# Two transformer layers with attention: dense products in column tiles, half of the first shifted copies on GpSimd

## The chip, the core and the metric

One core of one Trainium2 chip runs the whole program in one launch. The time is the device time of an execution in microseconds; the kernel before was timed three times.

## What is computed

Four blocks in a row on x of 2048 tokens by 512 features, in bf16: attention, a feed-forward network, attention, a feed-forward network, each on a layer norm of x and added to x. Both layers use the same weights.

```python
def _A_ref(x, wqkv, wo):                      # 32 heads of 16 features
    q, k, v = split((x @ wqkv))               # scale 16 ** -0.5
    p = softmax(einsum("bhqd,bhkd->bhqk", q, k) * scale)
    return merge(einsum("bhqk,bhkd->bhqd", p, v)) @ wo
def _B_ref(x, w1, b1, w2, b2):                # 512 -> 1376 -> 512
    y = _layernorm(x)
    return gelu(y @ w1 + b1) @ w2 + b2
x = x + _A_ref(_layernorm(x), wqkv, wo)
x = x + _B_ref(_layernorm(x), w1, b1, w2, b2)
# ... and both once more
```

## The kernel before

**Work.** The queries are cut into units of 512 tokens (the last unit of the second layer into 256, 128 and 128), the heads into 8 groups of four. A unit and a head group make a segment, and a segment is a list of score tiles: 128 keys by 512 queries of one head. One tile fills one PSUM bank of 512 f32 columns.

**TensorE's three forms.** A head has 16 features, padded to 32 rows, so a score product (L1536) uses 32 of the array's 128 rows: four heads run side by side as row tiles. A product of exponentials with V (L1741) has 17 columns, 16 features and a row of ones that sums the denominator: four heads run side by side as column tiles and add up in one bank. The dense products use the whole array: QKV (L1016), output projection (L1821), both feed-forward products (L1882, L1943), and in the tail the last unit's second feed-forward product (L2004). The planner charges a switch between the forms (`PE_SWITCH`). Products of zeros (L1425 whole array, L1427 rows, L1429 columns) fill gaps.

**Two ways to an exponential.** Scores are scaled and shifted beforehand so that the integer part of their value is the bit pattern of a bf16 exponential. ScalarE takes groups of three and of two banks in turn and writes exponentials PT (L1521). VectorE takes single tiles: it reads the bank, adds a constant and converts to 16-bit integers dp, which read as bf16 are a rough exponential (the load, L1628). Two such tiles make a batch, 128 x 1024. The error is evened out by four copies of it, shifted by 0, 32, 64 and 96 in the bits, each multiplied with its own weighted V (vs). The copies are made on VectorE: the first adds 32 to the batch (L1659, 128x1024), the second adds 64 to both (L1667, 128x2048). Where two batches are ready at once one instruction does both (L1614 and L1615). So a tile on VectorE leaves four products with V to TensorE, one on ScalarE leaves one.

**GpSimd (POOL)** scales queries (L1262), writes the weighted V (L1287), applies layer norms (L951), squares keys (L1057), computes softmax bounds (L1095 to L1099) and merges the two parts of segments that are done in halves (L1784, L1792 to L1795).

**What sets the order.** When the kernel is built, a planner (`Sched.run`) keeps a clock for each engine. Jobs submit tasks with priorities and estimated durations; `best` picks for each engine the ready task with the best priority, and the order so found is written out as fixed instruction streams with semaphores. Each engine then runs its stream in order. Scores have priority 0; `scores_due` holds other products back when scores come due. `take_d` decides which tiles go to VectorE, by how much work is waiting there and by free buffers; lanes are bank 5 (`DLANE`) and bank 7 (`MISCB`). `try_pv` sizes the blocks of products with V, at most `PV_DEEP` = 2 rounds. A string (`Hint.ORDER`) sets a few planner constants anew for every fourth score group. For GpSimd and VectorE sharing, the planner adds to a "fast" VectorE task a fixed amount for each GpSimd task that overlaps it (`hits`).

**The tail.** After the last scores the last unit of 128 tokens goes through `job_tail`: its projection, its norm, L1882 with gelu on ScalarE (L2024) chunk by chunk, and L2004.

Of the kernel before, what the change touches and what calls it, by code (L numbers as in the profile page):

```python
# [24 lines left out]
DMA_MARGIN = 1.0  # L25

# [5 lines left out]
EPS = 1e-5  # L32
# [31 lines left out]
class Prog:  # L64


    def __init__(self):
# [11 lines left out]
        self.hits = []  # L79
# [26 lines left out]
    def op(self, eng, fn, reads=(), writes=(), same_ok=(), dur=0.3, lat=None):  # L106
# [12 lines left out]
        op.t0 = max(self.free[eng], self.ready(eng, reads, writes, same_ok))  # L119
        if eng == "sp":  # L120
# [158 lines left out]
class Sched:  # L279
# [102 lines left out]
    def task_ready(self, t):  # L382
        P = self.P
        r = 0.0
        for (fn, reads, writes, same_ok, dur, lat) in t.ops:
            x = P.ready(t.eng, reads, writes, same_ok)
            if x > r:
                r = x
        return r

    def best(self, e):
# [102 lines left out]
HOLD_LEAD = 0.45  # L494
FILL_GAP = 0.2
# [22 lines left out]
PV_DEEP = 2  # L518
# [40 lines left out]
class Builder:  # L559
# [45 lines left out]
    def alloc(self, es):  # L605
# [21 lines left out]
        self.cneg = t("cneg", [128, 4], F32)  # L627
        self.chalf = t("chalf", [128, 1], F32)
# [130 lines left out]
    def build_startup(self):  # L759
# [29 lines left out]
        pool(lambda e: e.memset(self.cneg[:, :], -0.5), [("cneg",)])  # L789
        pool(lambda e: e.memset(self.chalf[:, :], 0.5), [("chalf",)])  # L790
# [137 lines left out]
    def ln_group(self, tiles, slot, prio, eps1, eps0, shift):  # L928
# [12 lines left out]
        yield Task("pool", prio, [I(lambda e: e.tensor_scalar(out=rs, in0=var, scalar1=eps1, scalar2=eps0, op0=ALU.mult, op1=ALU.add), [("mv", c0 + i) for i in range(n)], [R], 0.2),  # L941
# [1225 lines left out]
```

## Time and profile before

| what | value |
|---|---|
| median of 3 runs | 1535.7 us (1535.5 to 1536.29) |
| the profiled execution, its span | 1535.9 us |
| instructions | 41170 |
| TensorE (PE), VectorE (DVE), ScalarE (ACT), GpSimd (POOL) busy | 97%, 94%, 98%, 22% |
| granted TensorE clock, mean | 0.999 |
| first exponential of scores, last one | 21.6 us, 1520.1 us |
| data moved by DMA | 90.55 MB, 59 GB/s |

The profiled execution has no time outside its span that these runs show: span and median differ by 0.2 us. In the rows that follow, a group stands with its line, engine and operation, the tile written and the tiles read, partitions by elements, the count, busy microseconds and mean nanoseconds of one, and the engine's idle time just before such instructions with what ended it. Instructions of one engine overlap a little at their ends, so a sum of durations is more than the busy time. TensorE's busy time includes the products of zeros, so 97% doesn't mean that it has no room. In a list of waits each row has the total, the number and the longest, in us. In a timeline a row begins with its start and its length in us.

### The profile page before, as it was taken

How to read it: one execution, taken by the hardware profiler on the slowest of the kernel's cores; microseconds unless marked ns; L12 is line 12 of the kernel's file. 1: busy time of each engine (PE TensorE's matmuls, PEld its weight loads, DVE VectorE, ACT ScalarE, POOL GpSimd, SP SyncE). 2: the span in 40 equal slices, each digit the busy share in tenths (PEclk: the TensorE clock that was granted, in tenths of full speed). 3: DMA queues.
4: the chain of work that ended last, by engine and by line, in shares of the span. 5: the costliest groups of instructions: out<-in, count | busy, mean ns of one | idle time of the engine just before them, and what ended most of it. 6: DMA issues, size and time to landing. Idle time of an engine off the chain costs nothing.

```text
span 1535.9 us, 41170 instructions
## 1 busy us (share of the span) xinstructions
PE 1486.8 (97%) x17654; PEld 491.3 (32%) x17654; DVE 1442.2 (94%) x2661; ACT 1502.5 (98%) x1346; POOL 343.0 (22%) x570
## 2 busy tenths in 40 slices
PE   9999999999999999999999999999999999999998
PEld 3222222222222222222322332222222222344555
DVE  8799999999999999999999899999999989998786
ACT  8999999999999999999999999999999999999897
POOL 3576321102120022202322138220002000020110
PEclk9999999999999999999999999999999999999999
DMA  6663102213312123214842332210011001120221
GB/s 163 120 154 91 32 22 34 51 35 68 82 48 63 37 64 84 56 35 100 138 69 64 60 87 63 53 30 18 22 36 35 14 27 32 36 49 18 73 67 30
DMA packets 212487, 90.55 MB, mean 59 GB/s; under 512 B 182251, under 2 KB 207184, under 8 KB 212304
## 3 DMA queue, kind: packets, MB, share of 16 engines
q1 hardware_dynamic: 212304, 87.92, 25.6%
q8 instruction: 138, 2.26, 0.6%
q14 instruction: 45, 0.37, 0.1%
HBM read 36.81 MB, written 19.48 MB: 37 GB/s over the span
## 4 chain that ended last, share of the span: by engine, by line
ACT 44%; PE 27%; DVE 24%; issue 3%; POOL 2%; DMA 0%; DVEq 0%; POOLq 0%
ACT PT L1521 41%; DVE dp L1628 10%; PE ps L1536 9%; PE ps L1741 8%; PE ps L1943 3%; DVE dp L1667 3%; PE ps L1882 2%; PE ps L1016 2%; ACT h L1934 2%; DVE dp L1615 2%; DVE dp L1659 1%; PE ps L1425 1%; DVE accT L1771 1%; DVE st L933 1%; DVE dp L1614 1%
## 5 line engine op out<-in xcount | busy, mean ns | idle before, releaser
L1521 ACT ACTIVATE PT<-ps 128x1536 bf16<-128x1536 f32 (+1 forms) x1256 | 1422.0, 1309 | 20.6 <-PE ps L1536 18.8
L1628 DVE TENSOR_SCALAR dp<-ps 128x512 uint16<-128x512 f32 x979 | 648.8, 679 | 33.7 <-PE ps L1536 30.4
L1536 PE MATMUL ps<-QT,KT 32*128 32x512 bf16 (+2 forms) x5120 | 602.6, 340 | 23.9 <-ACT PT L1521 7.5
L1741 PE MATMUL ps<-PT,V 128*17 128x512 bf16 (+2 forms) x3899 | 491.1, 338 | 0.6 <-issue 0.5
L1741 PE MATMUL ps<-dp,vs 128*17 128x512 bf16 (+2 forms) x3663 | 460.8, 339 | 2.7 <-issue 1.8
L1536 PEld LDWEIGHTS ps<-QT,KT 32*128 32x128 bf16 x5120 | 174.1, 91 | 543.6 <-ACT PT L1521 297.6
L1262 POOL TENSOR_SCALAR QT<-qraw,scl,qbias 128x512 bf16<-128x512 bf16 (+2 forms) x91 | 75.2, 827 | 762.8 <-PE ps L1536 754.3
L1741 PE MATMUL ps<-dp,V 128*17 128x512 bf16 (+2 forms) x1221 | 232.3, 340 | 1.6 <-DVE accT L1771 1.2
L1667 DVE TENSOR_SCALAR dp<-dp 128x2048 uint16<-128x2048 uint16 x310 | 214.3, 694 | 4.9 <-PE ps L1741 1.8
L1741 PEld LDWEIGHTS ps<-dp,vs 128*17 128x17 bf16 x3663 | 124.1, 89 | 114.1 <-issue 84.8
L1741 PEld LDWEIGHTS ps<-PT,V 128*17 128x17 bf16 x3899 | 126.9, 89 | 94.2 <-issue 75.1
L1429 PE MATMUL ps<-zw 128*32 128x448 bf16 (+23 forms) x1514 | 147.1, 322 | 0.1
L1659 DVE TENSOR_SCALAR dp<-dp 128x1024 uint16<-128x1024 uint16 (+1 forms) x298 | 126.1, 426 | 2.6
L1427 PE MATMUL ps<-zw 32*128 32x444 bf16 (+7 forms) x386 | 119.5, 332 | 0.0
L1615 DVE TENSOR_SCALAR dp<-dp 128x4096 uint16<-128x4096 uint16 x91 | 111.0, 1225 | 0.6 <-PE ps L1741 0.4
L1882 PE MATMUL ps<-yT,wf 128*128 128x512 bf16 (+5 forms) x440 | 102.7, 340 | 2.1 <-issue 1.0
L1016 PE MATMUL ps<-wqkv,xnT 128*128 128x512 bf16 x336 | 91.7, 382 | 4.1 <-DVE h L1029 1.1
L1425 PE MATMUL ps<-zw 128*128 128x448 bf16 (+14 forms) x347 | 87.4, 338 | 4.4 <-DVE onec L809 2.1
L1287 POOL TENSOR_SCALAR vs<-V 128x340 bf16<-128x340 bf16 (+2 forms) x72 | 64.3, 894 | 23.0 <-PE ps L1741 16.2
L1741 PEld LDWEIGHTS ps<-dp,V 128*17 128x17 bf16 x1221 | 58.2, 89 | 34.6 <-issue 19.4
L1614 DVE TENSOR_SCALAR dp<-dp 128x2048 uint16<-128x2048 uint16 x97 | 67.8, 700 | 0.0
L1771 DVE STREAM_TRANSPOSE accT<-ps 128x512 f32<-128x512 f32 (+2 forms) x96 | 59.2, 617 | 5.3 <-PE ps L1741 5.0
(201 smaller groups left out, 1053.4 us busy)
## 6 DMA issues: line engine op xcount, KB each, us to landing
vs<-vs_scr SPq DMA_DIRECT2D x64, 255.0 KB, 2.8
wf<-in_B_w_dram SPq DMA_DIRECT2D x90, 128.0 KB, 2.5
q_scr<-qk SPq DMA_DIRECT2D x20, 256.0 KB, 2.0
k_scr<-qk SPq DMA_DIRECT2D x12, 256.0 KB, 2.1
out_dram<-xres SPq DMA_DIRECT2D x16, 128.0 KB, 1.7
vs_scr<-vs SPq DMA_DIRECT2D x8, 255.0 KB, 3.3
xres<-in_A_x_dram SPq DMA_DIRECT2D x7, 256.0 KB, 5.3
v_scr<-vst SPq DMA_DIRECT2D x12, 136.0 KB, 1.7
```

The lines of the kernel that those rows point to most:

```text
L1016: yield Task("pe", prio if c0 == 0 else min(prio, HINT.LIN2), [I(lambda e, c=c: e.matmul(self.ps[:, b, :], lhsT=xnT[:, c, :], rhs=self.wqk ...
L1425: fn = lambda e: e.matmul(self.ps[:, b, 0:w], lhsT=self.zw[:, 0:128], rhs=self.zw[:, 0:w], start=st, stop=st, skip_group_check=True)
L1427: fn = lambda e: e.matmul(self.ps[:, b, 0:w], lhsT=self.zw[32 * p:32 * p + 32, 0:128], rhs=self.zw[32 * p:32 * p + 32, 0:w], start=st, sto ...
L1429: fn = lambda e: e.matmul(self.ps[32 * p:32 * p + 32, b, 0:w], lhsT=self.zw[:, 0:32], rhs=self.zw[:, 0:w], start=st, stop=st, skip_group_c ...
L1521: S_.submit(Task("act", 1e-5 * gi, [I(lambda e, pt=pt, n=n, b0=b0: e.activation(out=self.PT[:, pt:pt + n, :], in_=self.ps[:, b0:b0 + n, :] ...
L1536: return [I(lambda e, kb=kb, i=i: e.matmul(self.ps[:, b, i * W:(i + 1) * W], lhsT=self.KT[32 * hp:32 * hp + 32, hg, kb * 128:(kb + 1) * 12 ...
L1615: return lambda e: e.tensor_scalar(out=self.both(x[1], y[1]), in0=self.both(x[0], y[0]), scalar1=float(SHIFT[2]), scalar2=None, op0=ALU.add)
L1628: self.S_.submit(Task("dve", 0.0, [I(lambda e: e.tensor_scalar(out=self.dpu(u)[:, w * 512:(w + 1) * 512], in0=self.ps[:, b, :], scalar1=BI ...
L1659: t = Task("dve", prio(), [I(lambda e: e.tensor_scalar(out=self.dpu(u + 1)[:, 0:N], in0=self.dpu(u)[:, 0:N], scalar1=float(SHIFT[1]), scal ...
L1667: t = Task("dve", prio(), [I(lambda e: e.tensor_scalar(out=self.dpp(v)[:, :, 0:N], in0=self.dpp(u)[:, :, 0:N], scalar1=float(SHIFT[2]), sc ...
L1741: ops.append((nth[j, sh] + 0.1 * i, I(lambda e, hp=hp, v=v, ap=ap[:, i * W:(i + 1) * W], first=first and i == 0, W=W: e.matmul(self.ps[32 ...
L1882: yield Task("pe", self.soft(pr if c0 == 0 else min(pr, HINT.LIN2)) if y0 == 0 else pr, [I(lambda e, c=c: e.matmul(self.ps[0:M, b, 0:W], l ...
```

## The change

Three things change in what is computed where, and the planner that orders all of it changes with them.

1. **Dense products as four column tiles.** A new function `dense` writes one product of 128x128 weights as four products with 32 columns of the weights each, in the column form of the products with V, into the four quarters of the same bank. QKV beyond the first four token tiles, the output projection and both feed-forward products use it. The tail's projection and its second feed-forward product stay whole.
2. **TensorE stays in column tiles while scores can wait.** When the best task is scores and TensorE is in column form, `stay` looks for a column task that ends, with a switch, before the scores are due, and takes that first. Blocks of products with V can be up to 4 rounds deep in some hint modes.
3. **First shifted copies on GpSimd.** `shifter` gives the first copy of a full batch to GpSimd when GpSimd is free within 1.5 us and the segment has at least 12 tiles left; such a copy adds a constant of two 16-bit halves as 32-bit integers. The planner starts it behind VectorE's last "fast" task ("after"), and models a shared port: a fast task of VectorE and the body of a GpSimd task shut each other out.

Durations of many tasks are set anew, more VectorE tasks count as fast, the last unit of the first layer gets a better priority behind its attention, and `Hint.ORDER` is a new string over more modes.

```diff
@@ Prog.op
-                self.hits = self.hits[-3:] + [(op.t0, op.t0 + dur, lat or 0.0)]
+                if lat == "after" and self.dve_port[1] is not None:
+                    order = self.dve_port[1]
+                    op.t0 = max(op.t0, order.t1 + LATENCY["pool"])
+                body = max(op.t0 + POOL_HEAD, self.dve_port[0])
+                dur = body + max(0.0, dur - POOL_HEAD) - op.t0
+                if lat != "brief":
+                    self.pool_port = (body, op.t0 + dur)
...
-                dur += sum(h for t0, t1, h in self.hits if t0 < op.t0 + dur and op.t0 < t1)
+                body = op.t0 + DVE_HEAD
+                if self.pool_port[0] <= body:
+                    body = max(body, self.pool_port[1])
+                dur = body + dur - DVE_HEAD - op.t0
+                self.dve_port = (op.t0 + dur, op)
@@ Sched.task_ready
+            if lat == "fast":
+                r = max(r, P.pool_port[1] - DVE_HEAD)
+            elif lat == "after":
+                r = max(r, P.dve_port[0] + LATENCY["pool"])
@@ Sched.best
+            if e == "pe" and HINT.DEFER > -1 and self.P.tiling == "col" and (b.ops[0][5] or ("full",))[0] == "row":
+                c = self.stay(f, lim)
+                if c is not None:
+                    return c
+    def stay(self, f, lim):
+        P = self.P
+        act = P.free["act"] + sum(max(0.02, o[4] - OVERLAP["act"]) for t in self.pend["act"] for o in t.ops)
+        dve = P.free["dve"] + sum(o[4] for t in self.pend["dve"] if self.task_ready(t) <= f + D_NEAR for o in t.ops)
+        due = min(act - HOLD_LEAD + HINT.DEFER, dve - STAY_LEAD)
+        if f > due - 0.2:
+            return None
...
+            if r <= lim and self.drained(t, max(f, r)) + PE_SWITCH <= due:
...
@@ Hint
-    BASE = dict(D_IDLE=1.2, PV_LEAST=0.75, HOLD_LATE=0.4, PV_NEAR=0.7, LIN2=9, D_STEAL=0, POST=0)
+    BASE = dict(D_IDLE=1.2, PV_LEAST=0.75, HOLD_LATE=0.4, PV_NEAR=0.7, LIN2=9, D_STEAL=0, POST=0, POOL_SHIFT=1, PV_DEEP=2, DEFER=0.0)
...
@@ Builder
+POOL_SHIFT_US = 1.037
...
+        self.cstep = t("cstep", [128, 1], I32)
...
+        pool(lambda e: e.memset(self.cstep.bitcast(U16)[:, :], SHIFT[1]), [("cstep",)])
@@ job_d
+        eng = self.shifter(sg, n)
...
+                                       lambda e: e.tensor_tensor(out=self.dpu(u + 1).bitcast(I32), in0=self.dpu(u).bitcast(I32), in1=self.cstep[:, 0:1].broadcast_to([128, 512]), op=ALU.add),
...
+    def shifter(self, sg, n):
+        S_ = self.S_
+        if n < DBATCH or not HINT.POOL_SHIFT or self.left(sg) < PURGE:
+            return "dve"
+        near = S_.now + POOL_NEAR
+        if self.P.free["pool"] > near or any(S_.task_ready(t) <= near for t in S_.pend["pool"]):
+            return "dve"
+        self.npool += 1
+        return "pool"
@@ oproj_mm, and alike in mm, mm_w1 and job_ffn
+        if K == 128 and not tail:
+            return Task("pe", pr, [o for hp in hps for o in self.dense(b, lambda w, hp=hp: self.OT[:, hp, i * 128 + w.start:i * 128 + w.stop], lambda hp=hp: self.wo[:, hp, :], [("OT", hp)] + [("wo", k) for k in range(8)], hp == 0, hp == 3)])
...
+    def dense(self, b, lhsT, rhs, reads, start, stop, M=128, W=512):
+        return [I(lambda e, j=j: e.matmul(self.ps[32 * j:32 * j + 32, b, 0:W], lhsT=lhsT(slice(32 * j, 32 * j + 32)), rhs=rhs(), start=start, stop=stop, skip_group_check=True, tile_position=(0, 32 * j)),
+                  reads, [("ps", b)], 0.216 * W / 512, [("ps", b)], ("col", j)) for j in range(M // 32)]
```

The order of instructions shows what comes of it. In its rows stand the line, the operation, the tile written and those read, and the shape; "x" counts repeats. Lines after the change are higher by 48 to 69: scores L1584, products with V L1803, dense quarters L1890, the load L1676, the first copy L1708 on VectorE and L1709 on GpSimd, the second L1717.

First place: TensorE at a second feed-forward product of the first layer (wf, h: weights and hidden rows; QT, KT: scores). Before:

```order
L1943 MATMUL ps<-wf,h 128x512 x10
L1943 MATMUL ps<-wf,g 128x512
L1741 MATMUL ps<-dp,vs 17x512 x4
L1741 MATMUL ps<-dp,V 17x512
L1741 MATMUL ps<-dp,vs 17x512 x3
L1536 MATMUL ps<-QT,KT 128x512 x4
L1943 MATMUL ps<-wf,h 128x512 x2
L1536 MATMUL ps<-QT,KT 128x512 x2
L1943 MATMUL ps<-wf,h 128x512 x2
```

At the same product TensorE has now:

```order
L1890 MATMUL ps<-wf,h 32x512 x40
L1890 MATMUL ps<-wf,g 32x512 x4
L1803 MATMUL ps<-dp,vs 17x512 x3
L1803 MATMUL ps<-dp,V 17x512
L1584 MATMUL ps<-QT,KT 128x512 x2
L1803 MATMUL ps<-dp,vs 17x512 x8
L1890 MATMUL ps<-wf,h 32x512 x8
L1584 MATMUL ps<-QT,KT 128x512 x3
L1890 MATMUL ps<-wf,h 32x512 x8
```

Ten whole products are forty quarters now, and the step from the dense block to the products with V is no change of form any more.

Second place: VectorE in the middle of the first layer, with the semaphores that each instruction waits for (s_pe, s_pool, s_dve: TensorE, GpSimd, VectorE itself). Before:

```order
L1614 TENSOR_SCALAR dp<-dp 128x2x1024
L1659 TENSOR_SCALAR dp<-dp 128x1024 [waits s_dve]
L1628 TENSOR_SCALAR dp<-ps 128x512 [waits s_pe]
L1615 TENSOR_SCALAR dp<-dp 128x2x2048 [waits s_dve]
L1628 TENSOR_SCALAR dp<-ps 128x512 [waits s_dve,s_pe]
L1667 TENSOR_SCALAR dp<-dp 128x2048
```

VectorE after the change, at about the same place:

```order
L1717 TENSOR_SCALAR dp<-dp 128x2048 [waits s_pool]
L1676 TENSOR_SCALAR dp<-ps 128x512 [waits s_pe]
L1979 TENSOR_SCALAR h<-ps,b1c 128x512 [waits s_pe]
L1676 TENSOR_SCALAR dp<-ps 128x512 [waits s_pe] x4
L1717 TENSOR_SCALAR dp<-dp 128x2048 [waits s_pe,s_pool]
L1676 TENSOR_SCALAR dp<-ps 128x512 [waits s_pe] x2
```

First copies (L1659, L1614) have left VectorE's stream here, and second copies wait for GpSimd, with loads behind them in the stream.

Third place: TensorE in the tail, behind the last scores (L2004 before, L2071 after: the second feed-forward product). Before:

```order
L2053 MATMUL ps<-ident,xn 128x128 x4
L1943 MATMUL ps<-wqkv,g 128x512
L1882 MATMUL ps<-yT,wf 128x128 x16
L2004 MATMUL ps<-wqkv,h 128x512
L1882 MATMUL ps<-yT,wf 128x128 x2
```

In the tail TensorE has now:

```order
L2120 MATMUL ps<-ident,xn 128x128 x4
L1890 MATMUL ps<-wqkv,g 32x512 x4
L1890 MATMUL ps<-yT,wf 32x128 x64
L2071 MATMUL ps<-wqkv,h 128x512
L1890 MATMUL ps<-yT,wf 32x128 x8
```

Here quarters and whole products alternate, so there are changes of form where there were none.

More of the change, by code (lines that the diff above doesn't have):

```diff
@@ L25 @@
 DMA_MARGIN = 1.0
+POOL_HEAD = 0.2
+DVE_HEAD = 0.137
 LOG2E = 1.4426950408889634
@@ L119, in op @@
         op.t0 = max(self.free[eng], self.ready(eng, reads, writes, same_ok))
+        order = None
         if eng == "sp":
@@ L162, in op @@
                 add_dep(d, w)
+        if order is not None:
+            deps[id(order)] = order
         op.deps = list(deps.values())
@@ L494 @@
 HOLD_LEAD = 0.45
+STAY_LEAD = -0.3
+PV_OPEN = 0.25
 FILL_GAP = 0.2
@@ L1056, in job_qkv_tile @@
         eng = "pool" if what == "kv" else "dve"
-        yield Task(eng, prio, [I(lambda e: e.tensor_tensor(out=sq, in0=v4, in1=v4, op=ALU.mult), [("qk", qs, k) for k in range(k0, k1)], SR, 0.14 + 0.00845 * N if eng == "dve" else 1.04)])
+        yield Task(eng, prio, [I(lambda e: e.tensor_tensor(out=sq, in0=v4, in1=v4, op=ALU.mult), [("qk", qs, k) for k in range(k0, k1)], SR, 0.14 + 0.00845 * N if eng == "dve" else 1.04, (), "fast" if eng == "dve" else None)])
         if "k" in what:
@@ L1658, in job_d @@
         prio = lambda: 0.15 if not self.left(sg) and sg is self.segs[self.acc_seg] else 0.5 if self.left(sg) < DURGE else 2.5
[L1659 to L1661 removed]
+        eng = self.shifter(sg, n)
+        t = Task(eng, prio() if eng == "dve" else 0.6, [I((lambda e: e.tensor_scalar(out=self.dpu(u + 1)[:, 0:N], in0=self.dpu(u)[:, 0:N], scalar1=float(SHIFT[1]), scalar2=None, op0=ALU.add)) if eng == "dve" else
+                                       lambda e: e.tensor_tensor(out=self.dpu(u + 1).bitcast(I32), in0=self.dpu(u).bitcast(I32), in1=self.cstep[:, 0:1].broadcast_to([128, 512]), op=ALU.add),
+                                     ([] if eng == "dve" else [("cstep",)]) + [("dp", u, w) for w in range(n)], [("dp", u + 1, w) for w in range(n)] + self.dres(u + 1), 0.150 + 0.2605e-3 * N if eng == "dve" else POOL_SHIFT_US, (), "fast" if eng == "dve" else "after")])
+        if n == DBATCH and eng == "dve":
             t.mate = (1, u, u)
@@ L1704, in try_pv @@
                 by[sg["tiles"][it[1]][1]].append(it)
-            value = lambda r: sum(min(r, len(v)) for v in by.values()) / (4.0 * (r + PV_COST))
-            r = max(range(1, PV_DEEP + 1), key=value)
+            cost = PV_OPEN if self.P.tiling == "col" and not self.pv_out else PV_COST
+            value = lambda r: sum(min(r, len(v)) for v in by.values()) / (4.0 * (r + cost))
+            r = max(range(1, HINT.PV_DEEP + 1), key=value)
             if value(r) < HINT.PV_LEAST and not self.starved and len(near) < sg["n"] - sg["sub"]:
```

84 lines of the change are left out of this document (45 added, 39 removed).

## The prediction

> **What bounds the kernel now.** I read the page first: its busy shares, the chain that ended last, and the costliest groups.
>
> ```profile
> span 1535.9 us, 41170 instructions
> ...
> PE 1486.8 (97%) x17654; PEld 491.3 (32%) x17654; DVE 1442.2 (94%) x2661; ACT 1502.5 (98%) x1346; POOL 343.0 (22%) x570
> ...
> ACT 44%; PE 27%; DVE 24%; issue 3%; POOL 2%; DMA 0%; DVEq 0%; POOLq 0%
> ...
> L1521 ACT ACTIVATE PT<-ps 128x1536 bf16<-128x1536 f32 (+1 forms) x1256 | 1422.0, 1309 | 20.6 <-PE ps L1536 18.8
> ```
>
> Three engines are above 90%. Which of them sets the time? The list of waits says:
>
> ```profile
> PEld ps L1536 <- ACT PT L1521: 297.6, 751, 0.8
> ...
> ACT PT L1521 <- PE ps L1536: 18.8, 48, 2.5
> ```
>
> TensorE waits 297.6 us for ScalarE to free score banks; ScalarE waits 18.8 us for scores. So ScalarE's exponentials set the pace, and the other engines matter where they make it wait or take tiles from it. Its rows, shapes apart:
>
> ```profile
> L1521 ACT ACTIVATE PT<-ps 128x1536 bf16<-128x1536 f32 x605 | 924.6, 1528 | 14.6 <-PE ps L1536 13.2
> L1521 ACT ACTIVATE PT<-ps 128x1024 bf16<-128x1024 f32 x651 | 712.5, 1105 | 5.9 <-PE ps L1536 5.7
> ```
>
> 605 exps of three banks and 651 of two are 3117 banks (tiles of 512 columns). Neighbouring exps overlap, so the price of a bank is the page's union: 1422.0 / 3117 = 0.456 us. The rest of the score tiles, 979 of them, go to VectorE. The stages differ:
>
> ```profile
> core 0: us, PE busy (x) PEld busy (x) DVE busy (x) ACT busy (x) POOL busy (x), PEclk, DMA share, GB/s
> 400.00:500.00 100.00, 98.70 (x948) 28.03 (x945) 98.79 (x174) 99.79 (x89) 18.63 (x33) 1.00 0.25 66
> ...
> 800.00:900.00 100.00, 98.63 (x955) 29.66 (x952) 90.69 (x165) 97.64 (x84) 22.64 (x39) 1.00 0.26 57
> ...
> 848.50:862.00 13.50, 13.50 (x103) 4.11 (x102) 6.94 (x12) 12.19 (x12) 0.00 (x0) 1.00 0.00 0
> ```
>
> Mostly ScalarE is over 99% busy. In a burst of dense products (848.5 to 862) TensorE is busy throughout, VectorE half idle, and ScalarE loses 1.3 us. ScalarE's waits in 39:200, 800:1000 and 1400:1521:
>
> ```profile
> ACT PT L1521 <- PE ps L1536: 3.9, 14, 0.6
> ...
> ACT PT L1521 <- PE ps L1536: 5.3, 10, 2.5
> ...
> ACT PT L1521 <- PE ps L1536: 5.2, 10, 2.1
> ```
>
> These three stages hold 14.4 of the 18.8 us.
>
> **Part 1: first shifted copies on GpSimd.** A batch of two tiles on VectorE is two loads (L1628), a first copy (L1659, or L1614 for two batches at once) and a second copy (L1667, L1615).
>
> ```profile
> L1628 DVE TENSOR_SCALAR dp<-ps 128x512 uint16<-128x512 f32 x979 | 648.8, 679 | 33.7 <-PE ps L1536 30.4
> L1667 DVE TENSOR_SCALAR dp<-dp 128x2048 uint16<-128x2048 uint16 x305 | 212.2, 699 | 4.9 <-PE ps L1741 1.8
> L1659 DVE TENSOR_SCALAR dp<-dp 128x1024 uint16<-128x1024 uint16 x293 | 124.7, 429 | 2.6
> L1615 DVE TENSOR_SCALAR dp<-dp 128x4096 uint16<-128x4096 uint16 x91 | 111.0, 1225 | 0.6 <-PE ps L1741 0.4
> L1614 DVE TENSOR_SCALAR dp<-dp 128x2048 uint16<-128x2048 uint16 x97 | 67.8, 700 | 0.0
> ```
>
> By the order of instructions 258 of some 490 full batches get their first copy from GpSimd. VectorE: loads +18 x 0.679 = +12.2; single first copies -144 x 0.429 = -61.8; joined ones -55 x 0.700 = -38.5; single second copies +50 x 0.699 = +35.0; joined ones -23 x 1.225 = -28.2; ten more short batches, at half of 0.429 + 0.699, +5.6. Sum -76 us: VectorE falls from 1442 to about 1366 us.
>
> What the end sees of this is only the tiles that leave ScalarE: 601 and 648 exps, 3099 banks, 18 fewer. **18 x 0.456 = -8.2 us.** The 76 us buy only 18 tiles because copies must now wait in turn; that is the cost side.
>
> GpSimd's new copy, 512 32-bit words with a broadcast second operand, is not in this trace. Near rows are a 16-bit product of 512 elements, and on f32 a product of 256 with a broadcast operand (L1792), an add of two full streams (L1795) and a product of 16 (L1793):
>
> ```profile
> L1057 POOL TENSOR_TENSOR h<-qk x2: 1035/1037/1039, 47.8 to 68.4; 128x512 bf16<-128x512 bf16 x2
> ...
> L1792 POOL TENSOR_TENSOR dp<-dp,dw x16: 614/621/1316, 108.9 to 974.4; 128x256 f32<-128x256 f32 x16
> ...
> L1795 POOL TENSOR_TENSOR accT<-accT,dp x16: 726/731/1775, 110.1 to 976.6; 128x256 f32<-128x256 f32 x16
> ...
> L1793 POOL TENSOR_TENSOR den<-den,dw x16: 214/220/1203, 109.4 to 975.5; 128x16 f32<-128x16 f32 x16
> ```
>
> From medians: broadcast, (621 - 220) / 240 = 1.67 ns an element, so 220 + 496 x 1.67 = 1.05 us; two streams, 2.13 ns, so 1.28 us. I take 1.05, the row of the same form, and keep 1.04 to 1.28. The plan in the code reckons with 1.037. GpSimd gets 258 x 1.05 = 271 us on top of 343, 40% of the span. It has room, but its queue is in order: query scaling, layer-norm rows and merges can wait one copy more. [...]
>
> The two engines also exclude each other. Fast VectorE copies against GpSimd's query scaling:
>
> ```profile
> 788.21 0.78 DVE L1659 TENSOR_SCALAR dp<-dp 128x1024 uint16<-128x1024 uint16 x1
> ...
> 787.94 0.77 POOL L1262 TENSOR_SCALAR QT<-qraw,scl,qbias 128x512 bf16<-128x512 bf16 x1 [13.20 <-PE ps L1536]
> ...
> 1333.84 1.28 DVE L1667 TENSOR_SCALAR dp<-dp 128x2048 uint16<-128x2048 uint16 x2
> ...
> 1333.87 1.60 POOL L1262 TENSOR_SCALAR QT<-qraw,scl,qbias 128x256 bf16<-128x256 bf16 x1 [10.69 <-PE ps L1536]
> ```
>
> At 788 GpSimd came first (ends 788.71) and the copy took 0.78 instead of 0.43. At 1333 the copies came first (end 1335.12) and GpSimd stretched to 1.60. So each of the 258 copies closes VectorE's fast copies out for up to a microsecond; loads from PSUM go on. The new order starts GpSimd right behind a fast copy and puts loads beside it, and 213 second copies wait outright for GpSimd. If one is late, the loads queued behind it wait, and TensorE waits for their lanes. With the order fitted to 1.037 I take +1 us at the end, bounds -1 (lanes free earlier) to +20 (rival C).
>
> **Part 2: dense products as four column tiles.** Around a dense burst:
>
> ```profile
> 847.32 2.33 PE L1943 MATMUL ps<-wf,h 128*128 128x512 bf16 x10
> 849.49 0.38 PE L1943 MATMUL ps<-wf,g 128*128 128x512 bf16 x1
> 849.80 0.40 PE L1741 MATMUL ps<-dp,vs 128*17 128x512 bf16 x4
> 850.02 0.38 PE L1741 MATMUL ps<-dp,V 128*17 128x512 bf16 x1
> ...
> 850.35 0.60 PE L1536 MATMUL ps<-QT,KT 32*128 32x512 bf16 x4
> ...
> 626.26 0.74 PE L1429 MATMUL ps<-zw 128*32 128x448 bf16 x12
> ```
>
> Ten dense products take 2.17, 0.217 each; four column tiles 0.22 (849.80 to 850.02); from one form to another 0.31 (849.49 to 849.80), so a switch costs 0.31 - 0.216 = about 0.095. The order has 2670 changes of form before and 2568 after: -102 x 0.095 = -9.7 us of TensorE, in the stages where ScalarE waits. Against it, 18 more VectorE tiles replace 18 products with V by 72: +54 / 4 x 0.22 = +3. Does a dense product keep 0.217 in quarters? Twelve zero products with 32-column weights run in 0.74: (0.74 - 0.36) / 2 = 0.19 a round for 448 columns. So yes. [...] Staying in column tiles while scores can wait (`stay`) moves scores late on purpose; they are still planned to land before ScalarE runs dry. Of the 14.4 us of waits I take **-3 us**, bounds -12 and +8.
>
> **Part 3: the tail.** Behind the last scores before, everything on TensorE has one form:
>
> ```profile
> 1527.38 1.07 PE L1882 MATMUL ps<-yT,wf 128*128 128x128 bf16 x16 [0.30 <-DVE yT L2055]
> ...
> 1528.28 0.38 PE L2004 MATMUL ps<-wqkv,h 128*128 128x512 bf16 x1
> 1528.49 0.28 PE L1882 MATMUL ps<-yT,wf 128*128 128x128 bf16 x2
> ```
>
> After, the first product is in column tiles and the second is not: 12 changes, 12 x 0.095 = 1.1, in a stretch where little hides it: **+1 us**. The step constant and the planner's new costs issue nothing that lies on the path: 0.
>
> **Sum.** -8.2 + 1 - 3 + 1 = -9.2 us. The profiled execution (span 1535.9) and the median of the runs (1535.7) differ by 0.2, so I predict **1526.5 us**.
>
> **Rivals.** Changes within 0.2% (3.1 us) can't be told from none.
> A, the forecast: 1519 to 1532.6. For it: ScalarE's rate is steady, and its instruction count is fixed by the order. Chance 0.62.
> B, the dense stages stop making ScalarE wait: -8.2 + 1 - 12 + 1 = -18.2, 1517.5. Against it: the longest waits (2.5, 2.1) look like chains at stage ends, not switches. Chance 0.10.
> C, slower: GpSimd's copy is nearer 1.28 than 1.037, and closes out the second copies. 258 x 0.24 = 62 us of lateness; if a third reaches ScalarE through lanes and scores, +20 instead of +1, and the dense waits don't shrink: -8.2 + 20 + 0 + 1 = +12.8, 1548.5. It decides from about a fifth of the 62 on, where 13 us use up the gain and 3.1 more. For it: the 213 direct waits, with loads queued behind them. Against it: the broadcast row and VectorE's freed 76 us. Chance 0.14. [...]
> D, the quarters don't keep pace: four weight loads of 0.095 one after another would make 0.38 of 0.217; the order has 4408 quarters of 512 columns, 1102 products, and 1102 x 0.163 = 180 us of TensorE where it is full; a third on the path gives 1526.5 + 60 = 1586. The row at 626.26 speaks against it. Chance 0.04.
>
> ```profile
> L1429 PEld LDWEIGHTS ps<-zw 128*32 128x32 bf16 x1514 | 53.0, 95 | 20.6 <-DVE dp L1628 2.8 <-issue 1.0 <-ACT PT L1521 0.8
> ```
>
> E, gains and new waits cancel: within 0.2%. Chance 0.10.
>
> **The numbers.** Faster is A and B, 0.72; same E, 0.10; slower C and D, 0.18. The range runs from 1513 (B with a little more) to 1541 (a C where some 12 us pass through); beneath lie 0.05, above about 0.13.
>
> **What would show it.** Right: exps 601 and 648, ScalarE busy near 1494; the new copy at 1.04 to 1.10; dense quarters at 0.22 a round; ScalarE's wait for scores about 16 us; VectorE busy below 1400. Wrong: VectorE's second copies waiting for GpSimd by more than 30 us, or ScalarE's wait for scores above 28.

## The result and the profile after

The changed kernel takes **1556.2 us** (median of 4 runs, 1552.1 to 1558.0), the kernel before 1536.0 beside it. The ratio is 1.0123, interval 1.0104 to 1.0142: slower by 1.2%, where 1526.5 was forecast, above the upper end of the range, 1541. The profiled execution has a span of 1553.9. Its page and two of its groups, in the columns that the prediction showed:

```profile
span 1553.9 us, 48864 instructions
...
PE 1486.7 (96%) x21441; PEld 516.9 (33%) x21447; DVE 1388.1 (89%) x2527; ACT 1499.9 (97%) x1339; POOL 602.6 (39%) x829
...
PE 32%; ACT 32%; DVE 23%; POOL 5%; issue 3%; DMA 2%; SPq 2%; POOLq 0%; DVEq 0%
...
L1569 ACT ACTIVATE PT<-ps 128x1536 bf16<-128x1536 f32 (+1 forms) x1249 | 1419.7, 1275 | 38.3 <-PE ps L1584 35.0
```

```profile
L1569 ACT ACTIVATE PT<-ps 128x1536 bf16<-128x1536 f32 x601 | 898.5, 1495 | 30.3 <-PE ps L1584 27.8
L1569 ACT ACTIVATE PT<-ps 128x1024 bf16<-128x1024 f32 x648 | 687.8, 1070 | 8.0 <-PE ps L1584 7.2
...
L1709 POOL TENSOR_TENSOR dp<-dp,cstep 128x512 int32<-128x512 int32 x258 | 268.1, 1039 | 662.7 <-DVE dp L1676 381.0 <-DVE dp L1717 163.0 <-DVE dp L1663 51.6
```

601 and 648 exps as forecast, and the new copy costs 1.039. But the exps' union fell by 2.3 us (1422.0 to 1419.7), not by 8.2: one exp now takes 1495 and 1070 where it took 1528 and 1105, because fewer of them start while the one before still runs (1128 instead of 1174, counted in the traces) and these overlap it by less (0.15 us instead of 0.19 on average). An exp that starts behind the end of the one before takes 1450 or 1024 ns in both traces. So scores that come a little later can leave no idle row and still cost overlap. VectorE shows the same: its instructions sum to 69 us less, its busy time falls by only 54, to 1388 and not 1366. ScalarE's share of the chain went from 44% to 32%. The list of waits says what else is late:

```profile
ACT PT L1569 <- PE ps L1584: 35.0, 63, 4.5
DVE dp L1676 <- PE ps L1584: 61.5, 88, 6.7
DVE dp L1717 <- POOL dp L1709: 5.8, 7, 1.2
```

ScalarE waits 35.0 us for scores (18.8 before; 16 was forecast), VectorE's loads 61.5 (30.4 before). VectorE's second copies wait only 5.8 us for GpSimd: rival C is not what happened.

Where was it lost? The order differs, so instants can't be compared, but work can: each of the 4096 score tiles is either a bank of an exp or a load on VectorE. Counting the ends of both in the two traces gives the time at which so many tiles were done, and how many of them VectorE did:

```
tiles done      930     1926    2092    2424    3752    4090   last exp   end
before, us    368.7    729.7   786.0   914.4  1381.0  1519.0    1521.2  1535.9
after, us     371.0    726.4   791.3   925.6  1389.9  1534.3    1537.1  1553.9
difference     +2.3     -3.3    +5.4   +11.2    +8.8   +15.3     +15.9   +18.0
VectorE's     202/205  442/459  484/489 556/561 901/920 979/997
```

At tile 1926 the change does what it should: 17 more tiles on VectorE, 3.3 us ahead. Then 14.5 us go between 725 and 925, where the second layer's attention begins (the third of the four blocks, called the third layer from here on), and 9 from tile 3752 to the end.

**Between 725 and 925.** The third layer's keys and values are reloaded from memory in SyncE's queue. The reload's rows of before and, in the second fence, of after:

```profile
740.51 9.30 SPq L1301 DMA_TRANSPOSE KT<-k_scr  x5
...
752.85 2.89 SPq L1303 DMA_DIRECT2D V<-v_scr  x2
```

```profile
761.70 7.55 SPq L1349 DMA_TRANSPOSE KT<-k_scr  x4
...
778.26 0.57 SPq L1351 DMA_DIRECT2D V<-v_scr  x1
...
786.45 8.13 SPq L1351 DMA_DIRECT2D V<-v_scr  x6
```

It begins 21 us later, though the exps are ahead. VectorE meanwhile runs almost dry (1.62 us busy in 12.2), and then GpSimd, TensorE and ScalarE wait in one chain. The columns are those of the prediction's table of stages; the first fence is of before at the same instants (though not at the same work), where VectorE is busy throughout, the others are of after:

```profile
771.00:783.20 12.20, 12.06 (x151) 3.71 (x148) 12.18 (x21) 12.20 (x12) 3.42 (x4) 1.00 0.65 102
...
800.00:820.00 20.00, 19.90 (x215) 5.88 (x216) 19.89 (x37) 19.98 (x18) 7.24 (x10) 1.00 0.27 62
```

```profile
771.00:783.20 12.20, 11.94 (x120) 4.55 (x120) 1.62 (x4) 11.35 (x11) 3.00 (x4) 1.00 1.08 182
...
800.00:820.00 20.00, 15.57 (x162) 3.92 (x162) 14.86 (x28) 14.65 (x14) 9.27 (x15) 0.83 0.28 66
```

```profile
808.60:812.00 3.40, 3.36 (x23) 0.55 (x23) 3.25 (x8) 2.18 (x2) 0.46 (x2) 0.50 0.34 77
```

```profile
803.40 2.28 POOL L1335 TENSOR_SCALAR vs<-V 128x204 bf16<-128x204 bf16 x3 [4.34 <-PE ps L1584]
805.63 0.40 POOL L1846 COPY dp<-accT 128x256 f32<-128x256 f32 x1
...
806.54 1.03 POOL L991 TENSOR_TENSOR rs<-rs,cneg 128x4 f32<-128x4 f32 x1
807.55 1.04 POOL L1709 TENSOR_TENSOR dp<-dp,cstep 128x512 int32<-128x512 int32 x1
```

```profile
808.64 0.60 PE L1803 MATMUL ps<-dp,vs 128*17 128x512 bf16 x2 [4.23 <-POOL dp L1709]
```

```profile
809.82 2.47 ACT L1569 ACTIVATE PT<-ps 128x1536 bf16<-128x1536 f32 x2 [4.51 <-PE ps L1584]
```

The shifted copy at 807.55 has no wait of its own. It stands in GpSimd's queue behind weighted values (L1335) that wait 4.34 us, and TensorE waits for the copy. After TensorE has stood, its granted clock is 0.50 from 808.6 to 812.0 (0.83 over the 20 us), and a product takes 0.60 instead of 0.38.

**Behind 1400.** Here the units have 256 and 128 tokens. TensorE's waits that nothing in the profile explains ("issue"), behind 1420 after, and in the second fence of before, behind 1405:

```profile
PE ps L1584 <- issue: 3.6, 4, 1.7
PE ps L1803 <- issue: 3.4, 5, 1.3
PE ps L1890 <- issue: 2.6, 4, 0.9
```

```profile
PE ps L1741 <- issue: 2.4, 2, 1.8
...
PE ps L1882 <- issue: 1.0, 1, 1.0
...
PE ps L1536 <- issue: 0.8, 1, 0.8
```

9.6 us in all against 4.2. Four of them, and the instructions of TensorE between two of them (products and weight loads with their counts):

```profile
1526.32 0.38 PE L1890 MATMUL ps<-yT,wf 128*32 128x128 bf16 x13 [0.94 <-issue]
...
1530.07 0.29 PE L1584 MATMUL ps<-QT,KT 32*128 32x128 bf16 x5 [0.69 <-issue]
...
1533.81 0.38 PE L1890 MATMUL ps<-yT,wf 128*32 128x128 bf16 x13 [0.85 <-issue]
...
1537.83 0.33 PE L1803 MATMUL ps<-PT,V 128*17 128x128 bf16 x9 [1.31 <-issue]
```

```profile
1530.10:1533.80 3.70, 2.86 (x128) 2.19 (x128) 2.49 (x8) 3.32 (x3) 0.00 (x0) 1.00 0.14 31
1533.80:1537.80 4.00, 2.71 (x128) 2.10 (x128) 0.92 (x3) 3.18 (x4) 0.00 (x0) 1.00 0.06 12
```

128 products and 128 weight loads each time, whatever the lines are: three times in a row TensorE stands after 256 instructions. Counted through TensorE's whole stream, all eight waits for issue over 0.6 us behind 1420 stand at the same place of successive 256s, to one instruction, and the 256 ahead of each had run in 2.5 to 3.3 us; one that ran in 3.04 us had no such wait. The four waits of the kernel before stand at one place too. No trace shows what TensorE waits for there: that it is for instructions is the author's estimate, from the place alone.

**Tail.** From the last exp to the end it takes 16.7 us, 14.6 before. Of these 2.1 us, 1.3 stand ahead of the first gelu, where ScalarE waits 4.91 us instead of 3.57, behind the wait for issue at 1537.83; the other 0.7 come between the chunks.

### The profile page after: what moved, and what is told of

Its sections match the earlier page's. It is cut to its first block, busy times and chain, and to the rows that moved or that the text cites. A ratio compares the mean times of both kernels' runs of the same rounds, so it can differ in the third digit from the quotient of the medians.

```text
span 1553.9 us, 48864 instructions
## 1 busy us (share of the span) xinstructions
PE 1486.7 (96%) x21441; PEld 516.9 (33%) x21447; DVE 1388.1 (89%) x2527; ACT 1499.9 (97%) x1339; POOL 602.6 (39%) x829
## 4 chain that ended last, share of the span: by engine, by line
PE 32%; ACT 32%; DVE 23%; POOL 5%; issue 3%; DMA 2%; SPq 2%; POOLq 0%; DVEq 0%
ACT PT L1569 30%; PE ps L1803 11%; PE ps L1584 11%; DVE dp L1676 10%; PE ps L1890 7%; DVE dp L1717 3%; POOL vs L1335 1%; DVE dp L1663 1%; PE ps L1477 1%; ACT h L2002 1%; DVE accT L1833 1%; DMA xnT<-xn 1%; DVE dp L1708 1%; DVE st L982 1%; PE ps L1473 1%
## 5 line engine op out<-in xcount | busy, mean ns | idle before, releaser
L1569 ACT ACTIVATE PT<-ps 128x1536 bf16<-128x1536 f32 (+1 forms) x1249 | 1419.7, 1275 | 38.3 <-PE ps L1584 35.0
L1676 DVE TENSOR_SCALAR dp<-ps 128x512 uint16<-128x512 f32 x997 | 659.8, 680 | 69.9 <-PE ps L1584 61.5
L1584 PE MATMUL ps<-QT,KT 32*128 32x512 bf16 (+2 forms) x5120 | 598.9, 341 | 27.4 <-DVE dp L1676 8.0
L1709 POOL TENSOR_TENSOR dp<-dp,cstep 128x512 int32<-128x512 int32 x258 | 268.1, 1039 | 662.7 <-DVE dp L1676 381.0
L1803 PE MATMUL ps<-PT,V 128*17 128x512 bf16 (+2 forms) x3878 | 501.6, 340 | 2.7 <-issue 2.4
L1803 PE MATMUL ps<-dp,vs 128*17 128x512 bf16 (+2 forms) x3726 | 483.9, 339 | 7.7 <-POOL dp L1709 4.9
L1584 PEld LDWEIGHTS ps<-QT,KT 32*128 32x128 bf16 x5120 | 172.4, 91 | 523.1 <-ACT PT L1569 257.9
L1717 DVE TENSOR_SCALAR dp<-dp 128x2048 uint16<-128x2048 uint16 (+1 forms) x370 | 253.1, 689 | 9.6 <-POOL dp L1709 5.8
L1803 PE MATMUL ps<-dp,V 128*17 128x512 bf16 (+2 forms) x1242 | 231.0, 340 | 2.7 <-DVE accT L1833 2.6
L1803 PEld LDWEIGHTS ps<-dp,vs 128*17 128x17 bf16 x3726 | 134.1, 89 | 138.3 <-issue 92.0
L1803 PEld LDWEIGHTS ps<-PT,V 128*17 128x17 bf16 x3878 | 134.9, 89 | 100.2 <-issue 78.6
L1477 PE MATMUL ps<-zw 128*32 128x448 bf16 (+17 forms) x1573 | 163.3, 329 | 0.1
L1475 PE MATMUL ps<-zw 32*128 32x444 bf16 (+3 forms) x391 | 122.1, 331 | 0.0
L1890 PE MATMUL ps<-yT,wf 128*32 128x512 bf16 (+2 forms) x1720 | 104.7, 339 | 5.9 <-issue 2.8
L1890 PE MATMUL ps<-wqkv,xnT 128*32 128x512 bf16 x1392 | 96.5, 381 | 3.8 <-DMA xnT<-xn 2.5
L1473 PE MATMUL ps<-zw 128*128 128x448 bf16 (+12 forms) x330 | 84.0, 340 | 4.0 <-DVE onec L858 2.1
L1663 DVE TENSOR_SCALAR dp<-dp 128x4096 uint16<-128x4096 uint16 x68 | 84.2, 1238 | 1.6 <-PE ps L1803 1.1
L1803 PEld LDWEIGHTS ps<-dp,V 128*17 128x17 bf16 x1242 | 59.5, 89 | 41.8 <-issue 17.6
L1335 POOL TENSOR_SCALAR vs<-V 128x340 bf16<-128x340 bf16 (+2 forms) x72 | 62.5, 869 | 21.0 <-DMA V<-v_scr 10.2
L1708 DVE TENSOR_SCALAR dp<-dp 128x1024 uint16<-128x1024 uint16 (+1 forms) x164 | 67.7, 418 | 1.1
```

Of the source, the lines that this page charges most:

```text
L1473: fn = lambda e: e.matmul(self.ps[:, b, 0:w], lhsT=self.zw[:, 0:128], rhs=self.zw[:, 0:w], start=st, stop=st, skip_group_check=True)
L1475: fn = lambda e: e.matmul(self.ps[:, b, 0:w], lhsT=self.zw[32 * p:32 * p + 32, 0:128], rhs=self.zw[32 * p:32 * p + 32, 0:w], start=st, sto ...
L1477: fn = lambda e: e.matmul(self.ps[32 * p:32 * p + 32, b, 0:w], lhsT=self.zw[:, 0:32], rhs=self.zw[:, 0:w], start=st, stop=st, skip_group_c ...
L1569: S_.submit(Task("act", 1e-5 * gi, [I(lambda e, pt=pt, n=n, b0=b0: e.activation(out=self.PT[:, pt:pt + n, :], in_=self.ps[:, b0:b0 + n, :] ...
L1584: return [I(lambda e, kb=kb, i=i: e.matmul(self.ps[:, b, i * W:(i + 1) * W], lhsT=self.KT[32 * hp:32 * hp + 32, hg, kb * 128:(kb + 1) * 12 ...
L1663: return lambda e: e.tensor_scalar(out=self.both(x[1], y[1]), in0=self.both(x[0], y[0]), scalar1=float(SHIFT[2]), scalar2=None, op0=ALU.add)
```

## Experiments

Two theories at the start. Theory 1, an assumption from the waits at every 256 instructions: quarters make TensorE's instruction stream too dense for its supply. Theory 2: the first copies sit in GpSimd's queue behind work that waits for a transfer. In all held-order runs the planner makes the same order, and the edit is applied to the finished list of instructions. Ratios are against the kernel before, run beside each.

**1. Quarters undone, in the order held.**

```
 def whole(ops):                        # on the finished order
+    four quarters of a group -> one matmul(ps[0:M, b, 0:W], ...)
     e1: where W < 512        e2: everywhere
```

> The changed kernel with its order held, but every dense product of 128 or 256 columns (the first products of the units of 256 and 128 tokens) issued whole again instead of as quarters: 132 fewer groups of four, 396 matmuls and 396 weight loads fewer, 11 more changes of form. Theory 1 (TensorE's instructions come in blocks of 256, and a block that runs in under about 3.5 us makes TensorE stand for about 1 us): the narrow quarters run through a block in about 2 us, so stalls over 0.6 us of TensorE behind 1420 fall from 10 to 5 or 6 and the kernel gains 3 to 6 us against the changed kernel, 1550 to 1553. Theory 2 (the time is lost where GpSimd's queue and late chains hold TensorE): no change by more than 2 us, 1554 to 1558.

> The changed kernel with its order held, but every dense product issued whole again. TensorE's instructions fall back to 17,694 products, changes of form rise from 2568 to 2816. Theory 1 in its wide form (the longer instruction stream costs everywhere): 5 to 12 us faster than the changed kernel, 1544 to 1551. Theory 2 (quarters are harmless and save changes of form): 248 x 0.095 = 24 us more TensorE time, of which a third to all comes through, 1563 to 1580.

e1: 1546.75, ratio 1.0067 (1.0050 to 1.0084). e2: 1552.66, 1.0102 (1.0075 to 1.0129). Theory 1 in its narrow form holds so far: 132 groups of quarters cost some 8 us, more than the 3 to 6 expected, and TensorE's waits for issue behind 1405 fall from 9.6 us to 2.0. The quarters' own work is not what costs: 64 narrow quarters take 1.08 us here, and the same 16 whole products took 1.07 (the prediction's row at 1527.38).

```profile
1544.61 1.08 PE L1890 MATMUL ps<-yT,wf 128*32 128x128 bf16 x64 [0.19 <-DVE yT L2122]
```

Theory 1's wide form isn't borne out: with the wide quarters gone too the kernel is slower than e1 by 0.35%, though the intervals overlap a little. Nor did e2 lose the 7 us or more that theory 2 gave it.

**2. Empty instructions in place of the quarters.**

```
-        ops[0][0].one = lambda e: e.matmul(...)
+        ops[0][0].one = lambda e: [e.nop() for _ in range(6)] and e.matmul(...)
```

> The changed kernel with its order held and narrow dense products whole, as before in the first experiment (1546.75), but six empty instructions ahead of each of the 132 whole products on TensorE, so that its instruction stream is as long as with quarters. Theory 1 (blocks of 256 instructions run dry): the stalls come back, 8 or more over 0.6 us behind 1420 about 3.5 us apart, and the kernel is back at 1553 to 1558. If it was the quarters' own work (weight loads, lanes, forms): it stays at 1545 to 1549. Should an empty instruction cost time of its own, TensorE's gaps grow by the same amount at each of the 132 places instead of in single stalls.

1549.36, 1.0083 (1.0057 to 1.0110). The trace has 48073 instructions, as in e1: none of the empty ones stands in it. If they did not reach the chip, this is e1 measured again, and it says nothing on the theory. So a longer stream without the quarters was not measured. Both together put the narrow quarters at 6 to 9 us in this order.

**3. Weighted values behind the copy.**

```
 def vs_behind_copy(ops):
+    three ops of L1335 and their store (L1342), planned ahead of the copy that runs at 807.55,
+    go behind that copy; nothing else moves
```

> The changed kernel with one move: the three weighted copies of V on GpSimd that wait for a late load near 803 us, and their store, stand behind the next layer-norm rows and the next shifted copy instead of ahead of them. Theory 2 (the shifted copy now sits in GpSimd's queue behind work that waits for a transfer, and TensorE and VectorE wait for it): ScalarE's wait of 4.51 at 809.82 goes below 1, TensorE's clock stays full there, and the kernel gains 4 to 7 us, 1549 to 1552. Theory 1 (instruction blocks): no change, 1554 to 1558. If something else is late by as much there, under 2 us gained.

1547.89, 1.0068 (1.0049 to 1.0087). The chain is cut:

```profile
800.78 1.04 POOL L1709 TENSOR_TENSOR dp<-dp,cstep 128x512 int32<-128x512 int32 x1
802.51 2.67 POOL L1335 TENSOR_SCALAR vs<-V 128x204 bf16<-128x204 bf16 x3 [0.69 <-DMA vs_scr<-vs]
```

```profile
810.14 4.62 ACT L1569 ACTIVATE PT<-ps 128x1536 bf16<-128x1536 f32 x4 [1.33 <-PE ps L1584]
```

ScalarE's 4.51 is gone, 1.33 is left, and the granted clock is 1.00 there. From tile 1926 to 2424 the kernel now takes 195.5 us instead of 199.2, so the place itself is worth 3.7; the rest of e3's 8 us is spread over the run. The row at 802.51 holds a hint: GpSimd's wait is here put down to the *store* of weighted values, not to a load.

**4. Quarters alone, in the order of before.**

```
 def four(ops):                         # before.py, on the finished order
+    one dense matmul -> four quarters
     e4: all        d1: where W < 512        d2: where W == 512
```

> The kernel before with its order held, and only the dense products issued as quarters: 17,654 products become 21,419, changes of form fall from 2670 to 2565. If quarters are a gain as the prediction has it (105 x 0.095 = 10 us of TensorE time, a third at the end): 1531 to 1535. Theory 1 in its narrow form (blocks of 256 run dry in the narrow units): the gain is eaten there, 1535 to 1540, with more stalls over 0.6 us behind 1400 than the 5 of before. Theory 1 in its wide form: slower, 1541 to 1550.

> The kernel before with its order held and only the narrow dense products (128 and 256 columns) as quarters. Changes of form 2673 against 2670, so nothing is saved. If narrow quarters cost time by running blocks of instructions dry: 1538 to 1542, with the loss behind 1400. If they cost only in the changed kernel's order: 1535 to 1538, no change.

> The kernel before with its order held and only the dense products of 512 columns as quarters. Changes of form 2564 against 2670: 106 x 0.095 = 10 us of TensorE time saved. If the 8 us that all quarters cost there (1544.49) was the narrow ones: 1531 to 1536. If the longer stream costs in the wide stretches too, or if what was saved there is worth nothing and late transfers come on top: 1538 to 1545.

e4: 1544.49, 1.0048 (1.0033 to 1.0062). d1: 1541.37, 1.0025 (1.0012 to 1.0037). d2: 1537.97, 1.0000 (0.9985 to 1.0014). This is the cleanest answer of the study: wide quarters save 106 changes of form, by the prediction's estimate of 0.095 each (from the rows at 849.49 and 849.80) 10 us of TensorE, and the kernel gains nothing; narrow ones save nothing and cost 0.25%. In d2 ScalarE waits 19.3 us for scores where it waited 18.8, and TensorE waits for ScalarE to free banks 312.0 us where it waited 297.6: where ScalarE sets the pace, TensorE's saved time has no taker.

```profile
PEld ps L1536 <- ACT PT L1521: 312.0, 783, 0.8
ACT PT L1521 <- PE ps L1536: 19.3, 42, 2.5
```

All quarters together cost 0.48%, more than the parts' 0.25% and nothing; where the rest comes from stays open.

**5. Both repairs, and all late dense products whole.**

```
 c1: whole (W < 512) and vs_behind_copy
 c2: whole (all dense products planned behind 1400) and vs_behind_copy
```

> The changed kernel with its order held and the two edits together: narrow dense products whole, and the late weighted V behind the shifted copy. If the two losses are separate, their gains add (9.5 and 8.3 us by medians): 1537 to 1541, level with the kernel before. If they are one chain seen twice, or if most of either was the spread of the runs: 1543 to 1547.

> The changed kernel with the late weighted V behind the copy, and every dense product behind 1400 of its order whole (not the narrow ones alone, as in the run with both edits, 1544.18): 289 products and weight loads fewer there, 7 more changes of form. If blocks that run dry still cost in that stretch: 1 to 4 us faster, 1540 to 1543. If the wide quarters are harmless there: 1543 to 1547.

c1: 1544.18, 1.0049 (1.0034 to 1.0064). The gains don't add: 11 us where the two alone gave 17 together. c2: 1538.44, 1.0003 (0.9990 to 1.0017): level with the kernel before. So the wide quarters, too, cost behind 1400. TensorE's waits for issue behind 1405 are 5.2 us in e3, 2.3 in c1 and 1.6 in c2. e3 still has all its quarters and less of these waits than the changed kernel (9.6), so they also move with small shifts of time. From e3 to c2 they give 3.6 us of a gain of 10, and from c1 to c2 0.7 of some 7, so how the wide quarters cost there is not shown. The rows of c2:

```profile
PE ps L1584 <- issue: 0.9, 1, 0.9
PE ps L1803 <- issue: 0.7, 3, 0.2
```

**6. First copies back on VectorE, in the order held.**

```
 def copies_on_dve(ops):
+    o.eng, o.spec = "dve", ("dve", o.fn.dve, ...)      # all 258
```

> The changed kernel with its order held, but all 258 first copies back on VectorE at the place that they have in the order. VectorE gets 258 x 0.43 = 111 us on top of 1388 and would be as full as ScalarE. If the copies on GpSimd are a gain as priced (part 1 of the prediction): 20 to 60 us slower than the changed kernel, 1575 to 1615. Rival C (GpSimd's copies hold everybody up, and the loss is theirs): faster than the changed kernel, below 1550.

1593.89, 1.0370 (1.0344 to 1.0396). Rival C falls: without GpSimd's copies this order is 2.4% slower. The order was laid out for them, so this is not what they are worth in an order of its own; f4, below, is nearer to that.

**7. Without the strings.**

```
-    ORDER = '57005f0fdfe00203h2...'
+    ORDER = ''            # f1 in before, f2 in after; f3: DEFER=-2.0; f4: POOL_SHIFT=0
```

> The kernel before with the string of planner modes emptied, so that every decision is made with the default knobs. It is the base for the next one. Slower than the kernel before by some per cent, 1570 to 1620; nothing in the traces gives a closer number.

> The changed kernel with the string of planner modes emptied, so that its three parts (quarters, staying, copies on GpSimd) stand without a string fitted to either side. If the parts lose by themselves: as slow as the emptied kernel before, or slower. If the parts gain and it is the new string's order that meets late transfers and full instruction blocks: faster than the emptied kernel before by 10 us or more.

> The changed kernel without a string, and with staying in column tiles turned off (1570.96 with staying). If staying pays: slower by 5 to 20 us, 1576 to 1591, with more changes of form (2731 against 2591: 140 x 0.095 = 13 us of TensorE time). If staying moves scores too late: faster, 1560 to 1569.

> The changed kernel without a string, and with no first copies on GpSimd (1570.96 with them, 328 of them). If the copies pay as the prediction priced them (VectorE's freed time buys tiles worth 8 us): slower by 4 to 12 us, 1575 to 1583. Rival C: faster, below 1568.

f1: 1602.42, 1.0435 (1.0414 to 1.0457). f2: 1570.96, 1.0226 (1.0208 to 1.0244). f3: 1585.20, 1.0317 (1.0298 to 1.0335). f4: 1575.01, 1.0249 (1.0231 to 1.0267). The prediction had no step for this: without strings the change's parts gain 31.5 us. Staying in column tiles is worth 14.2 of them and GpSimd's copies 4.0, each as expected ahead of its run; the other 13 were not taken apart. So the loss appears only with the strings in place. The old one is worth 66.2 us on the chip (1602.42 to 1536.23), the new one 14.8 (1570.96 to 1556.2).

**8. The reload, in the order held.**

```
 v1: the 16 reloads change places in SyncE's queue: K0 V0 K1 V1 V2 V3 K2 V4 ...
 v2: v1 and c2
 v3: v2, the stores of weighted values (L1342) right behind their computation,
     and the last three reloads behind the next four transposes (L1941)
```

> The changed kernel with its order held, except that the sixteen reloads of keys and values of the third layer are issued in the order in which they are first used: first keys, first values, second keys, second to fourth values, and so on, in the places that the sixteen have in SyncE's queue. If the late reload is what loses the stretch from 725 to 925 (first values issued at 778.27 behind seven key loads; VectorE idle from 771 to 783; the wait of 4.51 at 809.82): values land some 8 us earlier, VectorE is idle there for under 6 us, the wait of 4.51 is gone, 1542 to 1549. If only GpSimd's queue at 803 matters: as in the run with the weighted V moved, 1546 to 1550, with VectorE idle as before. If neither: 1554 to 1558.

> The changed kernel with all three edits: reloads in the order of their use, weighted V behind the copy, dense products behind 1400 whole. Without the first of them it was level with the kernel before (1538.44 against 1537.53). If the reload still costs the 7.6 us by which that kernel is behind at tile 2424: 1530 to 1535, faster than the kernel before. If it costs nothing more once the weighted V is out of the way: 1536 to 1540.

> As the kernel with three edits (1541.88), but in SyncE's queue the stores of the weighted values stand right behind their computation instead of behind all sixteen reloads, and the last three reloads, needed some 60 us later, stand behind the next four transposes. In the run with the loads in order of use, GpSimd waited 6.19 us at 804.26 for such a store. If that queue is what holds the place at 803 to 815: GpSimd's wait there is under 1 us, no wait of ScalarE over 1.5 us between 795 and 820, 1533 to 1538. If something else is late there: 1538 to 1543.

v1: 1551.42, 1.0105 (1.0088 to 1.0122). v2: 1541.88, 1.0042 (1.0029 to 1.0054), slower than c2. v3: 1537.68, 1.0011 (1.0002 to 1.0020). In v1 the values were issued at 763.40 instead of 778.26, VectorE stood idle all the same, and GpSimd waited longer than before:

```profile
771.00:783.20 12.20, 12.20 (x122) 4.56 (x120) 2.09 (x5) 11.35 (x11) 7.26 (x10) 1.00 0.87 125
...
800.00:820.00 20.00, 14.78 (x145) 4.05 (x145) 13.31 (x26) 12.96 (x12) 8.06 (x13) 0.83 0.38 87
```

```profile
804.26 2.28 POOL L1335 TENSOR_SCALAR vs<-V 128x204 bf16<-128x204 bf16 x3 [6.19 <-DMA vs_scr<-vs]
```

So the place had been read wrongly. The buffer for weighted values must be stored before it is filled again, and that store is queued behind the reloads (801.09 in v1, 797.77 in the changed kernel); the row at 803.40 had put the wait down to TensorE. With the stores first, GpSimd fills it at 803.27 without a wait:

```profile
802.15 1.04 POOL L1709 TENSOR_TENSOR dp<-dp,cstep 128x512 int32<-128x512 int32 x1
803.27 2.88 POOL L1335 TENSOR_SCALAR vs<-V 128x204 bf16<-128x204 bf16 x3
```

```profile
811.47 10.85 ACT L1569 ACTIVATE PT<-ps 128x1536 bf16<-128x1536 f32 x9 [1.29 <-PE ps L1584]
```

From v2 to v3 the stores (and the last three reloads) win 0.3%; against c2 nothing is gained. VectorE's idle time at 771 stays in all three (1.84 busy in v3), whenever the values are issued, so it most likely lies in the order, where its loads stand behind scores that come after 782.

**9. A string chosen under other costs.**

```
+        if W < 512 or self.S_.now > 1395.0: one whole matmul          # in dense
+            if op.t0 > 1380.0 and len(self.streams["pe"]) % 128 == 0: op.t0 = max(op.t0, self.block + 3.45)
-    KT reload 1.4, 1.7, 3.8   V reload 1.4, 1.2, 3.5                    # priority, issue, landing
+    KT reload 1.4 + 0.02 * hg, 2.0, 4.3   V reload 1.4 + 0.02 * hg, 1.4, 4.3
-    ORDER = '57005f0fdfe00203h2...'                                   # chosen anew from step 120 on
```

> The changed kernel with a string chosen anew from its 120th step on, by trying strings in the planner after four of its rules were changed: dense products are whole behind 1395 and where narrow; 256 instructions of TensorE take at least 3.45 us behind 1380; the third layer's reloads take 2.0 and 1.4 us of SyncE's queue and land half a microsecond to a microsecond later; keys and values of one group are asked for together. If the new string's order loses because its costs don't know these things: 1533 to 1543, 13 us or more faster than the changed kernel, with VectorE busy in the stretch where the third layer begins. If its order is no better for knowing them: 1546 or more.

1546.48, 1.0062 (1.0048 to 1.0076): 0.6% better than the changed kernel, but no more than the whole late products alone can explain (0.65% in experiment 5), and it falls in the range that was expected if the order is no better for knowing them. So this theory isn't borne out. Behind 1400 it loses nothing more against the kernel before (9.6 us behind at tile 3752, 6.1 at 4090). At the third layer its loss has only moved: it falls behind by 7 us between tiles 1594 and 1926, before the reload, and by 2 from there to 2424. No version that was run beats the kernel before.

## Why the prediction was wrong

The prediction said that the change saves 9.2 us, and it cost 20. What failed first is the third term of its sum, the dense quarters. Next come the argument that GpSimd's queue has room, the size of ScalarE's term, and a premise that the sum never states: that the new order suits the chip as well as the old one. Of its own signs of being wrong one came true, ScalarE's wait for scores above 28 (35.0).

- **ScalarE's term, -8.2: mis-sized.** 3099 banks came as counted, but priced at 0.456 each they were priced with the overlap of before. The union gave 2.3, because the exps overlap less.
- **GpSimd's copies, +1: the price right, the queue wrong.** 1.039 for 1.05; loads from PSUM went on beside it as said, 11 that ran wholly inside such a copy took 0.687 us on average, the 448 beside no work of GpSimd 0.680; VectorE's wait for them 5.8 us, far below rival C's 30; taking them away costs some 37 us in this order (h1) and, without strings, 4.0 (f4). The prediction said that query scaling, layer-norm rows and merges "can wait one copy more". It is the other way round: the copy waits for them, and TensorE for the copy. One such place, at 803, cost 8 us by e3's median alone, but only 3 on top of e1 (c1). By the tiles done from 1926 to 2424 it is 3.7 in e3 and 3.6 in c1 (198.8 us in e1, 195.2 in c1).
- **Dense quarters, -3: the step that failed.** The pace is as said, four rounds of quarters in 1.05, so (1.05 - 0.38) / 3 = 0.22 a round:

```profile
786.66 1.05 PE L1890 MATMUL ps<-wo,dp 128*32 128x512 bf16 x16 [0.31 <-DVE dp L1676]
```

  Rival D is out. But "-102 changes of form = -9.7 us of TensorE, of which -3 is taken" is worth 0 at the end (d2), and the number that mattered, the instructions, was not in the sum: 3787 products and as many weight loads more. Behind 1400, where the products are short, the quarters cost 10 us instead of saving: from e3 to c2, which differ in the late dense products alone, it is 0.65%. That the narrow ones cost through the instructions is supported by e1 (waits for issue 9.6 us to 2.0, time 9.5 us less); for the wide ones the way stays open, since these waits show only a part of it.
- **Staying, counted with the quarters:** right in sign, 14.2 us without a string.
- **The tail, +1:** +2.1, and the term was about right. ScalarE's two short waits there are 1.06 and 1.05 in the changed kernel and 0.62 each in v3, whose tail has whole products and takes 14.5 us from the last exp: 0.9 us for the changes of form, where 1.1 was taken. The other 1.3 come from ahead, by the wait for issue at 1537.83; no term had it. (c2's tail, also with whole products, takes 15.8 us, with a wait of 1.26 for a transfer.)
- **What no step had:** the string. The prediction took the new order, without saying so, to be as well fitted to the chip as the old one. On the chip the old string is worth 66 us and the new one 15 (f1, f2). Part of why is shown: with the copy out of the way of the late weighted values and the late products whole, the very same order is level with the kernel before (c2, v3). The rest, the forecast gain itself, stays open: VectorE's 11 idle us at 771 seem to be in the order itself, a string chosen under costs that know reload and blocks lost as much around the third layer's begin (g1), and why neither order passes it as cheaply as the old one is not settled.
- **The rivals:** the result lies beyond C's 1548.5, by none of the mechanisms named.

## What to carry to other kernels

Time saved on an engine that wasn't the bound was worth nothing here (an estimated 10 us of TensorE, ratio 1.0000 in d2), while what came with it, more instructions and longer in-order queues, cost: 0.65% where products are short and crowd (e3 to c2), 3.7 us where a copy stood behind a wait of 4.34 us (e3, tiles 1926 to 2424). Before moving work to an idle engine, list what stands ahead of it in that queue and what transfer that waits for. A string or table fitted to a planner's costs is a part of the change: measure both sides without it as well.

## What the hardware showed that we had not expected

- Behind 1420 TensorE's waits of 0.6 to 1.7 us that nothing in the profile explains all stand at one place of successive 256 instructions of its queue, behind stretches of 256 that ran in 2.5 to 3.3 us. Products of 128 columns with their weight loads run that fast (2.86 and 2.71 us busy).
- After TensorE's wait of 4.23 us that ends at 808.64 its granted clock was half (0.50 from 808.6 to 812.0, 0.60 us a product instead of 0.38), so this wait was paid twice.
